# A gated mix of a state-space layer and a GELU layer: the opening's ScalarE table load and parameter rows are re-placed, and four loads are cut into pieces

## The chip, the cores and the metric

The kernel runs on one core of one Trainium2 chip. A core has five engines that run side by side and meet at semaphores: TensorE (PE in the profile; its weight loads are PEld), VectorE (DVE), ScalarE (ACT), GpSimd (POOL) and SyncE (SP). ScalarE and SyncE also issue DMA transfers, each into a queue of its own; "ACTq" and "SPq" are these issues in the profile. The metric is the device time in microseconds, the median of 9 runs of the kernel before: 217.02 us (216.68 to 217.1).

## The reference

Tokens `x` (2048 x 640, bfloat16) go through two branches, and a sigmoid gate per token mixes them. Branch A is a diagonal state-space layer: project the tokens to 640 complex states, scan over time, project back, add a skip. Branch B is a dense layer with tanh-GELU, 640 to 1728 to 640.

```python
x = A_x
g = _sigmoid((x * gate_w).sum(-1, keepdims=True))
# branch A
dt = jnp.exp(log_dt)
Lam_bar = jnp.exp(dt * Lam)
B_bar = ((Lam_bar - 1.0) / Lam)[:, None] * Bmat
Bu = jnp.einsum("bld,pd->blp", x + 0j, B_bar)
# for every t:  h = Lam_bar * h + Bu[:, t]
a = 2.0 * jnp.einsum("blp,dp->bld", hseq, Cmat).real + x * Dskip
# branch B
b = _gelu(x @ w1 + b1) @ w2 + b2
return g * a + (1 - g) * b
```

`log_dt`, `Lambda_re` and `Lambda_im` are the three parameter rows (640 values each) that the change is about.

## The kernel before, in words

The 2048 tokens are worked on in four chunks of 512, and a chunk in four strips of 128 tokens. All matmuls have 128 rows to contract, so the 640 features are five blocks (`KD`), the 640 states five (`KS`) and the 1728 hidden units thirteen full blocks and a rest of 64 (`KF` = 14).

**Main stages.** `ff1(c)` multiplies chunk c by `w1` (L251 through `ff1_mm`), and ScalarE takes the GELU (L256). `ssm(c)` multiplies it by B (L534); ScalarE copies the result out (L537) and VectorE does the rotation and the scan (L469, L488). `fin_b(c)` multiplies by `w2` (L592; the last 64 hidden units in L608, which read a transposed tile `gelL`), and `fin_a(c)` multiplies the scanned states by C (L651), after `seed` has put `x * Dskip` into the bank (L567). VectorE combines both into an output strip `ot` (L656), which SyncE stores (L665, the last one L663 on two queues). The list of calls at L670 to L694 sets the order of the chunks' stages. For TensorE, VectorE and ScalarE the order from line 168 on is the order in which the code is written (`manual_schedule`). What stands above line 168, and SyncE's queue throughout, is put in order by the framework, by priority and by a model of when things are ready: the load of token rows 2, written behind `fin_a(0)`, is issued in the trace behind the first of that stage's four stores.

**The opening.** Chunk 0 is not loaded transposed. Its four strips are loaded as they are (`load_xn(0, ...)`, L119, SyncE), TensorE turns each by a multiplication with the identity (`turn`, L216; five 128 x 128 blocks a strip), and VectorE (L223) and ScalarE (L225) copy the result into `xT[0]`. Of each strip VectorE copies blocks 0 to 2 and ScalarE blocks 3 and 4; these last two always go through the same PSUM bank, `pA`. So the next strip's blocks 3 and 4 can be written only when ScalarE has copied the strip before. Between the strips TensorE already multiplies what it has by the first columns of `w1` (`strip`, L251). `w1` comes as `w1a` (the first six blocks of hidden units; one tile for each of five feature blocks, of which ScalarE's queue loads feature blocks 0 and 2 and SyncE's the others) and `w1b` (the rest).

**Parameter rows.** Three small transfers of five rows of 128 values (`rows`, L125) put `log_dt`, `Lambda_im` and `Lambda_re` into the tile `prmA`, which VectorE has cleared. One matmul with the identity (L327, into `pA`, behind the twelfth `w1a` matmul of the opening's second round) turns them into columns, VectorE copies these into `colA` (L328), and from there a chain over ScalarE and VectorE makes the step dt, the angles and the sine and cosine tables (L329 to L422). The rows for b1 and the gate go into `prmB` by SyncE and are turned at L389.

**ScalarE's tables.** A function that is not in ScalarE's active table costs a table load. The kernel has three: for exp (asked for by a one-element activation on the tile `warm`, L210), for sine (L377) and for gelu (L256).

**Loads behind the opening.** SyncE issues, in this order, the `w1b` blocks (L143), B, chunk 1 and C as DMA transposes (L154 to L158), `w2` as one transfer of 2080 KB (L159), its last rows, the biases, chunks 2 and 3 as DMA transposes and the token rows of chunk 1 (L166, 640 KB). The token rows of chunks 2 and 3 are loaded later, by one transfer of 640 KB each, once the tile that they overwrite has been read.

Of the kernel before, what the change touches and what calls it, by code (L numbers as in the profile page):

```python
# [11 lines left out]
ACT = mybir.ActivationFunctionType  # L12
BF16 = mybir.dt.bfloat16
F32 = mybir.dt.float32
I32 = mybir.dt.int32

P = 128
# [6 lines left out]
KS = D // P  # L24
KF = (F + P - 1) // P
F_LAST = F - (KF - 1) * P
NT = T // P
TPC = CH // P
H = TPC // 2
# [12 lines left out]
def kernel(  # L42
# [19 lines left out]
    nc = tc.nc  # L62
# [4 lines left out]
    const = ctx.enter_context(tc.tile_pool(name="const", bufs=1))  # L67
# [7 lines left out]
    def bank(dtype=F32):  # L75
        return ps.tile([P, CH * 4 // (4 if dtype == F32 else 2)], dtype, name="bank")
# [7 lines left out]
    w2_sb = const.tile([P, KF - 1, D], BF16, name="w2_sb")  # L84
# [6 lines left out]
    prmA = const.tile([P, P], BF16, name="prmA")  # L91
# [23 lines left out]
    def load_xn(c, a0=0, a1=TPC, queue=None):  # L115
        if a0 == 0:
            xn[c] = xnp.tile([P, TPC, D], BF16, name="xn")
        r0 = c * CH + a0 * P
        (queue or nc.sync).dma_start(out=xn[c][:, a0:a1, :], in_=x2d[r0:r0 + (a1 - a0) * P, :].rearrange("(a p) d -> p a d", p=P))  # L119

    def load_w1a(queue, kd):
        queue.dma_start(out=w1a[kd][:], in_=B_w1[kd * P:(kd + 1) * P, 0:cut1])

    def rows(queue, dst, v):
        queue.dma_start(out=dst, in_=v.rearrange("(j p) -> j p", p=P))  # L125
# [2 lines left out]
    load_w1a(nc.scalar, 0)  # L128
    load_xn(0, 1, 2)
    load_w1a(nc.scalar, 2)  # L130
    load_xn(0, 2, 3)
    nc.vector.memset(prmA[:], 0.0)
    nc.vector.memset(prmB[:], 0.0)
    rows(nc.scalar, prmA[0:KS, :], A_log_dt)
    rows(nc.scalar, prmA[KS:2 * KS, :], A_Lambda_im)
    rows(nc.scalar, prmA[2 * KS:3 * KS, :], A_Lambda_re)
    load_xn(0, 3, 4)
    for kd in (1, 4, 3):
        load_w1a(nc.sync, kd)
    rows(nc.sync, prmB[KS:NB, :], B_b1[0:(KF - 1) * P])  # L140
# [15 lines left out]
    nc.sync.dma_start_transpose(out=xT[1][:], in_=x2d[CH:2 * CH, :])  # L156
    nc.sync.dma_start_transpose(out=CT_re[:], in_=A_C_re[:, :])
    nc.sync.dma_start_transpose(out=CT_im[:], in_=A_C_im[:, :])  # L158
    nc.sync.dma_start(out=w2_sb[:, 0:KF - 1, :], in_=B_w2[0:(KF - 1) * P, :].rearrange("(kf p) d -> p kf d", p=P))  # L159
    for h in range(2):  # L160
        nc.sync.dma_start(out=w2l[h * F_LAST:(h + 1) * F_LAST, :], in_=B_w2[(KF - 1) * P:F, :])
    nc.sync.dma_start(out=b2bc[:], in_=B_b2.rearrange("(o d) -> o d", o=1).to_broadcast([P, D]))
    nc.sync.dma_start(out=Dbc[:], in_=A_Dskip.rearrange("(o d) -> o d", o=1).to_broadcast([P, D]))
    nc.sync.dma_start_transpose(out=xT[2][:], in_=x2d[2 * CH:3 * CH, :])
    nc.sync.dma_start_transpose(out=xT[3][:], in_=x2d[3 * CH:4 * CH, :])
    load_xn(1)  # L166

    ctx.enter_context(tc.manual_schedule(engines={E.PE, E.DVE, E.Activation}))

# [36 lines left out]
    tf = const.tile([P, HC], F32, name="tf")  # L206
    nc.vector.tensor_copy(out=tf[:], in_=tfi[:])
    ones = lambda n: nc.const_aps.tensor(1.0, [P, n], BF16)
    warm = const.tile([P, 1], F32, name="warm")
    nc.scalar.activation(out=warm[:], in_=ones(1), func=ACT.Exp)  # L210
    pA = bank()
    for n in (512, 512, 512, 512, 512, 512, 128, 128):
        nc.tensor.matmul(pA[:, 0:n], lhsT=ones(P), rhs=ones(n), start=True, stop=True)
# [311 lines left out]
    def ssm(c, at={}):  # L525
        hs[c] = hsp.tile([P, 2 * KS, CH], BF16, name="hs")
        for ks in range(KS):
            if ks in at:
                at[ks]()
            bu = work.tile([P, 2, CH], BF16, name="bu", bufs=8)  # L530
            for ri, BT in enumerate((BT_re, BT_im)):
                p = bank()
                for kd in range(KD):
                    nc.tensor.matmul(p[:], lhsT=BT[ks >= KSA][:, kd, (ks % KSA if ks < KSA else ks - KSA) * P:][:, 0:P], rhs=xT[c][:, kd, :],  # L534
                                     start=(kd == 0), stop=(kd == KD - 1))
                    pe(CH)
                nc.scalar.activation(out=bu[:, ri, :], in_=p[:], func=ACT.Identity)  # L537
                act(0.6)
            scan_ops(c, ks, bu, ck.act)
            if c == 0 and ks == 0:  # L540
                later(0, 1.6, factors)
            let_out(ck.pe)
# [42 lines left out]
    def first_banks(c):  # L585
        biased(c, "wide", 0)
        biased(c, "wide", 1)
# [49 lines left out]
    def fin_a(c, at={}):  # L637
        let_out(0, c)
        for a in range(TPC):
            ti = c * TPC + a  # L640
            lo = a * P
            ot = fwork.tile([P, D], BF16, name="ot", bufs=2)
            if a < TPC - 2:
                seed(ti + 2)
            if a in at:
                at[a]()
            for i, (d0, d1) in enumerate(cuts(ti)):
                p = seeded[ti][i]
                for j in range(2 * KS):
                    CT = CT_re if j < KS else CT_im  # L650
                    nc.tensor.matmul(p[:, 0:d1 - d0], lhsT=hs[c][:, j, lo:lo + P], rhs=CT[:, j % KS, d0:d1],  # L651
                                     start=False, stop=(j == 2 * KS - 1), skip_group_check=True)
                    pe(d1 - d0)

                def f():
                    nc.vector.scalar_tensor_tensor(out=ot[:, d0:d1], in0=p[:, 0:d1 - d0], scalar=gcol[:, 0, ti:ti + 1],  # L656
                                                   in1=gbs[ti][:, d0:d1], op0=ALU.mult, op1=ALU.add)

                dve_now(ck.pe + 0.2, 0.45, f)
                if ti == NT - 1 and i > 0:  # L660
                    s0 = 0 if i == 1 else d0
                    q = nc.sync if i == 1 else nc.scalar
                    q.dma_start(out=out2d[ti * P:(ti + 1) * P, s0:d1], in_=ot[:, s0:d1])  # L663
            if ti < NT - 1:
                nc.sync.dma_start(out=out2d[ti * P:(ti + 1) * P, :], in_=ot[:])  # L665
# [12 lines left out]
    ff1(2, 0, {1: lambda: fold(3), 4: lambda: fold(4), 9: lambda: seed(0), 11: lambda: seed(1)})  # L678
    gates(2)
    fin_a(0)  # L680
    load_xn(2)
    ssm(2, {KS - 1: lambda: first_banks(1)})
    fin_b(1, seeds(1))
    fin_a(1)
    load_xn(3)
    ssm(3)
    gel_tile(3)
    ff1(3, 0, {KF - 3: lambda: first_banks(2)})
# [36 lines left out]
```

## Time and profile before

| what | value |
|---|---|
| median of 9 runs | 217.02 us |
| the profiled execution, device time | 216.84 us |
| its span, first to last instruction | 215.1 us |
| granted TensorE clock | 1.000 |
| TensorE: first matmul, first matmul on data (L216), last matmul's end | 0.77, 3.54, 211.7 us |
| DMA, mean over the span | 74 GB/s |
| DMA, 2.4 to 4.8 us | 332 to 380 GB/s |

From issue to landing, by tile: a strip of 160 KB took 3.3 to 3.6 us, a `w1a` block of 192 KB 2.7 to 3.6, a `w1b` block of 240 KB 3.4 to 5.9, `w2` 10.0, token rows of 640 KB 4.7 in the median.

How to read it: a busy share is an average over the span. What an edit is worth is read from the place that it touches, and there from the wait that ends last. "Idle before" in square brackets is the engine's idle time ahead of that instruction, with the work that ended it.

### The profile page before, as it was taken

How to read it: one execution, taken by the hardware profiler on the slowest of the kernel's cores; microseconds unless marked ns; L12 is line 12 of the kernel's file. 1: busy time of each engine (PE TensorE's matmuls, PEld its weight loads, DVE VectorE, ACT ScalarE, POOL GpSimd, SP SyncE). 2: the span in 40 equal slices, each digit the busy share in tenths (PEclk: the TensorE clock that was granted, in tenths of full speed). 3: DMA queues.
4: the chain of work that ended last, by engine and by line, in shares of the span. 5: the costliest groups of instructions: out<-in, count | busy, mean ns of one | idle time of the engine just before them, and what ended most of it. 6: DMA issues, size and time to landing. Idle time of an engine off the chain costs nothing.

```text
span 215.1 us, 3548 instructions
## 1 busy us (share of the span) xinstructions
PE 210.2 (98%) x1385; PEld 116.6 (54%) x1385; DVE 190.1 (88%) x396; ACT 101.1 (47%) x183; POOL 1.1 (0%) x12
## 2 busy tenths in 40 slices
PE   7999999999999999999999999999999999999993
PEld 4745444454454644775445677444445477654773
DVE  2799999999999999898999999999999999983252
ACT  2599556675876696203563210456682423204200
POOL 1000000000000000000000000000000000000000
PEclk9999999999999999999999999999999999999999
DMA  6899999990000000061000005100000000110011
GB/s 206 271 199 223 231 232 359 195 229 12 3 0 0 3 2 0 12 186 61 0 0 3 0 8 191 48 2 0 0 5 12 0 3 30 61 34 0 0 64 63
DMA packets 30323, 15.84 MB, mean 74 GB/s; under 512 B 22882, under 2 KB 30306, under 8 KB 30306
## 3 DMA queue, kind: packets, MB, share of 16 engines
q1 hardware_dynamic: 29844, 15.18, 28.3%
q10 hardware_dynamic: 462, 0.43, 0.6%
q8 instruction: 11, 0.18, 0.3%
q14 instruction: 6, 0.05, 0.1%
HBM read 7.48 MB, written 2.62 MB: 47 GB/s over the span
## 4 chain that ended last, share of the span: by engine, by line
PE 96%; DMA 1%; ACT 1%; DVE 0%; ACTq 0%; issue 0%
PE bank L592 26%; PE bank L251 26%; PE bank L651 20%; PE bank L534 20%; DMA xn<-in_A_x_dram 1%; PE bank L608 1%; PE bank L277 1%; ACT L210 1%; PE bank L216 0%; DVE ot L656 0%; ACT xT L225 0%; ACTq L125 0%; ACT warm L210 0%; PE bank L267 0%; PE bank L389 0%
## 5 line engine op out<-in xcount | busy, mean ns | idle before, releaser
L592 PE MATMUL bank<-w_sb,gel 128*128 128x512 bf16 (+1 forms) x416 | 57.9, 299 | 0.0
L592 PEld LDWEIGHTS <-gel 128*128 128x128 bf16 x416 | 32.2, 98 | 25.5
L537 ACT ACTIVATE bu<-bank 128x512 bf16<-128x512 f32 x40 | 23.9, 597 | 38.9 <-PE bank L534 38.8
L256 ACT ACTIVATE gel<-bank,colB 128x512 bf16<-128x512 f32 x52 | 34.0, 695 | 11.8 <-PE bank L251 11.1
L651 PEld LDWEIGHTS <-hs 128*128 128x128 bf16 x330 | 31.6, 98 | 11.5
L488 DVE TENSOR_TENSOR_SCAN g<-r_c,carry,v 128x512 bf16<-128x512 f32 x30 | 37.4, 1271 | 0.0
L600 ACT ACTIVATE gb<-bank,gcol 128x512 f32<-128x512 f32 (+1 forms) x32 | 15.1, 527 | 34.3 <-PE bank L608 18.1
L251 PE MATMUL bank<-xT,w1b 128*128 128x512 bf16 x140 | 31.0, 379 | 0.0
L251 PE MATMUL bank<-xT,w1a 128*128 128x512 bf16 (+1 forms) x156 | 27.4, 330 | 0.0
L651 PE MATMUL bank<-CT_re,hs 128*128 128x320 bf16 (+2 forms) x165 | 27.1, 295 | 0.0
L651 PE MATMUL bank<-CT_im,hs 128*128 128x320 bf16 (+2 forms) x165 | 27.1, 295 | 0.0
L656 DVE SCALAR_TENSOR_TENSOR ot<-bank,gcol,gb 128x320 bf16<-128x320 f32 (+2 forms) x33 | 17.5, 533 | 9.9 <-PE bank L651 8.7
L534 PE MATMUL bank<-xT,BT_im 128*128 128x512 bf16 x100 | 24.8, 379 | 0.0
L534 PE MATMUL bank<-xT,BT_re 128*128 128x512 bf16 x100 | 24.8, 379 | 0.0
L251 PEld LDWEIGHTS <-w1b 128*128 128x128 bf16 x140 | 13.7, 98 | 16.4
L251 PEld LDWEIGHTS <-w1a 128*128 128x128 bf16 x156 | 13.4, 98 | 12.5
L567 DVE TENSOR_TENSOR bank<-xn,Dbc 128x320 f32<-128x320 bf16 (+2 forms) x33 | 14.5, 480 | 2.8 <-ACT gb L600 2.7
L534 PEld LDWEIGHTS <-BT_im 128*128 128x128 bf16 x100 | 9.8, 98 | 11.8
L469 DVE TENSOR_TENSOR v<-wa,wb 128x512 bf16<-128x512 bf16 x40 | 15.2, 420 | 0.6
L534 PEld LDWEIGHTS <-BT_re 128*128 128x128 bf16 x100 | 9.7, 98 | 11.0
L581 ACT ACTIVATE bank<-b2bc 128x512 f32<-128x512 bf16 (+1 forms) x24 | 11.7, 529 | 7.0 <-DVE ot L656 7.0
L469 DVE TENSOR_TENSOR wa<-TCOS,g 128x1024 bf16<-128x1024 bf16 x20 | 13.7, 685 | 0.1
(100 smaller groups left out, 151.0 us busy)
## 6 DMA issues: line engine op xcount, KB each, us to landing
out_dram<-ot SPq DMA_DIRECT2D x15, 160.0 KB, 1.8
w_sb<-in_B_w_dram SPq DMA_DIRECT2D x1, 2080.0 KB, 10.0
xn<-in_A_x_dram SPq DMA_DIRECT2D x3, 640.0 KB, 4.7
w1b<-in_B_w_dram SPq DMA_DIRECT2D x5, 240.0 KB, 4.5
xn<-in_A_x_dram SPq DMA_DIRECT2D x4, 160.0 KB, 3.5
w1a<-in_B_w_dram SPq DMA_DIRECT2D x3, 192.0 KB, 2.9
w1a<-in_B_w_dram ACTq DMA_DIRECT2D x2, 192.0 KB, 3.3
w2l<-in_B_w_dram SPq DMA_DIRECT2D x2, 80.0 KB
```

Of the source, the lines that this page charges most:

```text
L251: nc.tensor.matmul(p[:, t0:t1], lhsT=w, rhs=xT[c][:, kd, t0:t1], start=(kd == 0) if first is None else first, stop=(kd == last), skip_grou ...
L256: nc.scalar.activation(out=gel[c][:, kf, :], in_=p[:, :], func=ACT.Gelu_apprx_tanh, bias=b1_c[:, kf:kf + 1])
L469: nc.vector.tensor_tensor(out=o, in0=a, in1=b, op=op)
L488: nc.vector.tensor_tensor_scan(s["g"][:, ri, :], r_c[:, ks:ks + 1].to_broadcast([P, CH]), s["v"][:, ri, :], init, ALU.mult, ALU.add)
L534: nc.tensor.matmul(p[:], lhsT=BT[ks >= KSA][:, kd, (ks % KSA if ks < KSA else ks - KSA) * P:][:, 0:P], rhs=xT[c][:, kd, :], start=(kd == 0 ...
L537: nc.scalar.activation(out=bu[:, ri, :], in_=p[:], func=ACT.Identity)
L567: dve_now(ck.pe, 0.45, lambda: nc.vector.tensor_tensor(out=p[:, 0:d1 - d0], in0=xn[c][:, a, d0:d1], in1=Dbc[:, d0:d1], op=ALU.mult))
L581: nc.scalar.activation(out=v, in_=src, func=ACT.Identity)
L592: nc.tensor.matmul(p[:, col:col + d1 - d0], lhsT=gel[c][:, kf, a * P:(a + 1) * P], rhs=w2_sb[:, kf, d0:d1], start=False, stop=False, skip_ ...
L600: nc.scalar.activation(out=gbs[ti][:, d0:d1], in_=p[:, col:col + d1 - d0], func=ACT.Identity, scale=gcol[:, 1, ti:ti + 1])
L651: nc.tensor.matmul(p[:, 0:d1 - d0], lhsT=hs[c][:, j, lo:lo + P], rhs=CT[:, j % KS, d0:d1], start=False, stop=(j == 2 * KS - 1), skip_group ...
L656: nc.vector.scalar_tensor_tensor(out=ot[:, d0:d1], in0=p[:, 0:d1 - d0], scalar=gcol[:, 0, ti:ti + 1], in1=gbs[ti][:, d0:d1], op0=ALU.mult, ...
```

## The change

Three things are changed.

- The one-element exp activation that calls up ScalarE's first table stands behind ScalarE's two `w1a` loads; it stood at line 210, behind the three parameter rows.
- The three parameter rows are issued by SyncE, behind the fourth strip and ahead of its `w1a` blocks; they were issued by ScalarE.
- `w2` comes in four transfers (blocks 0 to 2, 3 to 5, 6 to 8 and 9 to 12), and the token rows of chunks 1, 2 and 3 in two halves each. Six transfers are added in all, each of them on SyncE's queue; the bytes are the same.

```diff
     load_w1a(nc.scalar, 0)
     load_xn(0, 1, 2)
     load_w1a(nc.scalar, 2)
+    warm = const.tile([P, 1], F32, name="warm")
+    nc.scalar.activation(out=warm[:], in_=nc.const_aps.tensor(1.0, [P, 1], BF16), func=ACT.Exp)
     load_xn(0, 2, 3)
     nc.vector.memset(prmA[:], 0.0)
     nc.vector.memset(prmB[:], 0.0)
-    rows(nc.scalar, prmA[0:KS, :], A_log_dt)
-    rows(nc.scalar, prmA[KS:2 * KS, :], A_Lambda_im)
-    rows(nc.scalar, prmA[2 * KS:3 * KS, :], A_Lambda_re)
     load_xn(0, 3, 4)
+    rows(nc.sync, prmA[0:KS, :], A_log_dt)
+    rows(nc.sync, prmA[KS:2 * KS, :], A_Lambda_im)
+    rows(nc.sync, prmA[2 * KS:3 * KS, :], A_Lambda_re)
     for kd in (1, 4, 3):
         load_w1a(nc.sync, kd)
...
-    nc.sync.dma_start(out=w2_sb[:, 0:KF - 1, :], in_=B_w2[0:(KF - 1) * P, :].rearrange("(kf p) d -> p kf d", p=P))
+    for k0, k1 in ((0, 3), (3, 6), (6, 9), (9, KF - 1)):
+        nc.sync.dma_start(out=w2_sb[:, k0:k1, :], in_=B_w2[k0 * P:k1 * P, :].rearrange("(kf p) d -> p kf d", p=P))
...
-    load_xn(1)
+    for a in (0, H):
+        load_xn(1, a, a + H)
...
-    warm = const.tile([P, 1], F32, name="warm")
-    nc.scalar.activation(out=warm[:], in_=ones(1), func=ACT.Exp)
...
     fin_a(0)
-    load_xn(2)
+    load_xn(2, 0, H)
+    load_xn(2, H, TPC)
...
     fin_a(1)
-    load_xn(3)
+    load_xn(3, 0, H)
+    load_xn(3, H, TPC)
```

## The prediction

> **What bounds the kernel now.** I read the page first, for the shares of the engines and the chain that ended last:
>
> ```profile
> PE 210.2 (98%) x1385; PEld 116.6 (54%) x1385; DVE 190.1 (88%) x396; ACT 101.1 (47%) x183; POOL 1.1 (0%) x12
> ...
> PE 96%; DMA 1%; ACT 1%; DVE 0%; ACTq 0%; issue 0%
> ```
>
> TensorE (PE) is busy for 210.2 of the 215.1 us. The stretches of the span show the rest: 0.77 us before its first matmul, 3.4 us after its last (211.7 to 215.1), which leaves about 0.73 us idle in between. Whatever does not move TensorE's work cannot move the end. Next, the chain of waits in order of time, to find those 0.73 us:
>
> ```profile
> 3.52 0.26 ACTq L125
> 3.78 0.03 issue
> 3.81 1.28 ACT L210
> 5.09 0.01 issue
> 5.11 0.20 ACT warm L210
> 5.31 0.28 ACT xT L225
> 5.59 0.04 issue
> 5.63 0.27 PE bank L216 x2
> ```
>
> Before these lines the chain holds the first token strip's transfer (0.72 to 3.49). From there to 5.63 it runs over ScalarE: the issue of the third parameter row (L125), which waited for that strip; behind it the table load (1.28 us), the warm-up and the copy of the first strip's transposes (L225). The timelines of ScalarE, then of TensorE, show what stands in line there and who waits for it:
>
> ```profile
> 1.66 0.57 ACTq L125 DMA_DIRECT2D prmA<-in_A_log_dt_dram  x1
> 2.26 0.27 ACTq L125 DMA_DIRECT2D prmA<-in_A_Lambda_im_dram  x1
> 3.52 0.26 ACTq L125 DMA_DIRECT2D prmA<-in_A_Lambda_re_dram  x1
> 3.81 1.28 ACT L210 ACT_TABLE_LOAD   x1 [3.81 <-DMA xn<-in_A_x_dram]
> 5.11 0.20 ACT L210 ACTIVATE warm<-const-bfloat16-1.0 128x1 f32<-128x1 bf16 x1
> 5.21 0.36 ACT L225 ACTIVATE xT<-bank 128x256 bf16<-128x256 f32 x1
> ```
>
> ```profile
> 4.57 0.34 PE L216 MATMUL bank<-ident,xn 128*128 128x128 bf16 x3
> 5.63 0.27 PE L216 MATMUL bank<-ident,xn 128*128 128x128 bf16 x2 [0.72 <-ACT xT L225]
> 5.74 0.83 PE L251 MATMUL bank<-xT,w1a 128*128 128x128 bf16 x12
> 6.41 0.17 PE L327 MATMUL bank<-ident,prmA 128*128 128x15 bf16 x1
> ```
>
> The reader is to see one stall of 0.72 us: TensorE, ready at 4.91, may not write the second strip's transposes into `pA` before ScalarE has copied the first strip's out of it. That is practically all of TensorE's idle time. The last line matters as much: L327 turns the three parameter rows into columns, and TensorE stands there in order until all three rows have landed.
>
> **The table load moves.** ScalarE's two `w1a` issues end at 1.62 (0.72 plus 0.90). Table load at 1.65 to 2.93, warm-up 2.95 to 3.15: over before the first strip's transposes finish at 4.23 (3.54 plus 0.69), so nothing waits for it; the cover is the wait for the first strip. The copy L225 then runs at 4.27 to 4.63 and is done before TensorE wants `pA`: three transposes of the second strip start at 4.57, one each 0.063 us, so the next two start at 4.76 and end 0.27 later, at 5.03. ScalarE copies them at 5.07 to 5.45. Without anything else L327 could come when 12 matmuls are issued; the last six of them need the first of VectorE's two copies (L223, two from 4.95 in 0.62, so about 5.25 to 5.3) and take half of the 0.67 us that lies between 5.74 and 6.41. That gives 5.63 instead of 6.41: 0.78 us earlier.
>
> On a table load row and rule differ. In this trace the load takes 1.28 us and the warm-up follows 0.02 us behind. The Trainium skill ("ScalarE: Activation LUTs", section "What ACT_TABLE_LOAD costs") counts a drain of about 1.38 us on top, 2.66 in all. By that figure ScalarE would be free at about 4.5, the first copy would end at about 4.9, and L327 would be possible some 0.15 later: still not what decides, by the next part.
>
> **The three rows move to SyncE.** ScalarE loses three issues (0.57, 0.27, 0.26 us), all hidden or gone with the stall. SyncE issues its four strips from 0.72 to 2.54 and stood idle until 3.69, as its timeline shows:
>
> ```profile
> 0.72 1.82 SPq L119 DMA_DIRECT2D xn<-in_A_x_dram  x4
> 3.69 1.65 SPq L122 DMA_DIRECT2D w1a<-in_B_w_dram  x3
> ```
>
> Rows one and two fit in that hole: 2.58 to 3.15 and 3.2 to 3.47. The third cannot be issued at once. The semaphore numbers in the DMA records cycle over eight, and an issue waits for the transfer that had its number eight issues before: that is why the third row waited for strip one, and why SyncE's first `w1a` issue waited 1.1 us for the `w1a` block that ScalarE had asked for (landed 3.68 by its completion events). With six issues on SyncE ahead of them the third row takes that place: I expect it at 3.69 to 3.95. Behind it in SyncE's queue the first `w1a` block slips 0.3 us (to 3.99); the next ones do not, since the second waited for strip two anyway (landed 4.52, issued 4.54). The slipped block lands at 6.4 to 6.8 and is first read after 9 us. Everything SyncE issues later, the b1 and gate rows, `w1b` and the transposes, keeps its time.
>
> Landing of the third row: before, issued at 3.52, its completion events end at 5.67, so 2.15 us. Issued at 3.69 it lands at 5.85. Bounds: its packets now stand behind strip four on the same queue, whose completions come at 5.17 to 5.70; on ScalarE's queue the rows landed one after another at 4.92, 5.30 and 5.67, about 0.37 apart. If a further such step comes on top, 6.2; if the path is a little quicker, 5.6. From landing to matmul it was 0.04 and 0.05 us for strip one, so L327 at 5.95, with 5.65 to 6.32 as ends. I take 5.95, nearest to the like row. So TensorE gives back about 0.3 of the 0.78 us as a new wait at L327.
>
> **Sum.** 6.41 minus 5.95 is 0.46 us. From L327 on the work is linked: VectorE's `colA` copy, the next write to `pA`, dt, the table chain (8.64, 10.0, the sine table load, 12.4), then the gelu table load and the first gelu, all follow it. Strips three and four (landed 5.32 and 5.70) are wanted at 6.1 and 7.3. So I shift all by 0.46. What does not shift are transfers. The nearest is the fifth `w1b` block: issue at 8.0, longest landing 5.9, so 13.9, and its weights were loaded at 14.54; after the shift 14.08. Covered by 0.17; if that cover is gone, at most 0.3 us come back. Next come the first matmuls of `ssm(0)` at 21.5 whose four B transposes land at 15.1 to 21.1 by their completion events, each 4 us and more ahead of its use.
>
> **More pieces.** `w2` in four issues instead of one: three more of 0.59 us on SyncE at 29 to 31. The whole block landed 10.0 us after 29.00 and is first read at 57.5. Behind it on SyncE stand `w2l`, the bias, Dskip, two transposes, token rows 1 and the first gelu transpose; they slip 2 us and a few more where an issue now waits for a `w2` piece. The earliest user is L608 at 64.75, with its transpose issued at 44.4. So nothing: it would take a slip of 10 us and more before a us of it is seen. Token rows of chunks 2 and 3 in halves: one more issue of 0.39 us each at 92.4 and 128.9, and an output store that may slip by as much. VectorE already waits for such a store (0.63 us at 97.29); TensorE does not wait for VectorE there, and no matmul there starts closer than 0.8 us behind the work it needs. If that cover were gone, 0.4 us each. I take nothing. The skill speaks against pieces ("DMA: Bandwidth & Descriptors", "Rules for kernel authors": at least 1 MiB per transfer for bandwidth). In this trace 160 and 192 KB transfers moved 332 to 380 GB/s between 2.4 and 4.8 us; and even at half the rate of before (an estimate) `w2` would land by 49 to 50, ahead of 57.5: nothing by either.
>
> The profiled execution took 216.84 us (span 215.1, 1.7 around it): 216.84 minus 0.46 is 216.38. It lies 0.18 under the median of 217.02, so the median becomes **216.56 us**.
>
> **Rivals.**
> *The rows are in time.* L327 at 5.63 to 5.7, gain 0.72 to 0.78, 216.24 to 216.3. For it: two rows are out by 3.5. Against it: the third needs another 2.15 us from 3.69.
> *The wait moves to the rows or to `w1b`.* The rows land a step late each, or `w1b` eats the rest: gain 0 to 0.1 or a loss of 0.2; 216.9 to 217.2. For it: the 0.37 steps above, and strip four ahead in the queue. Against it: those rows were shared with a queue full of strips, and theirs is nearly empty after 5.
> *Slower: the table load gets ahead of ScalarE's issues.* The schedule is pinned only from line 168 on. If load and warm-up stand before the first `w1a` issue, that block lands up to 1.5 us later, at 5.2; the third row, which waits for it, lands 2.15 later, 7.35; L327 at 7.45, 1.05 later than now: 218.1. Between the two issues it costs about 0.5. It decides as soon as the first issue starts after about 2. For it: SyncE's order is not the code's (token rows 2 stand after four stores in the code and are issued behind the first). Against it: ScalarE's five issues stand in code order in the trace.
> *It does not do what it says* is the second rival with the stall at 4.91 unchanged: only if the load stayed behind a wait for a strip.
>
> **Chances.** Forecast 0.60 (own range 216.2 to 216.95), rows in time 0.14, moved wait 0.12, slower 0.14. About 0.2%, 0.43 us, can be told from no change: faster means under 216.59. The forecast lies just below that line, so 0.33 of its 0.60, plus 0.14: 0.47. Same: 0.27 plus 0.12. Slower 0.14. The range goes from 216.15, full gain and a little, to 217.2, the end of the moved wait; the slower rival stays out.
>
> **What would show it.** Table load at about 1.65; no ScalarE wait at L216; a new TensorE wait of about 0.3 us ahead of L327 put down to a row's transfer; L327 near 5.95; the second gelu stage shifted alike, and TensorE's last matmul near 211.2. It is wrong if L327 comes after 6.3, if a wait appears at `w1b` near 14, or if any matmul after 27 us waits for a transfer or VectorE.

## The result, and the profile after

The changed kernel takes **216.23 us** (median of 10 runs, 215.81 to 216.77), against 216.97 us for the kernel before (median of 30). The ratio is 0.9969, with a 95% interval of 0.9961 to 0.9977: faster by 0.31%. The forecast was 216.56, with a range of 216.15 to 217.2 that holds the time. Its profiled execution took 216.08 us, span 214.3 (before 216.84 and 215.1), so 0.76 us are to be found.

The chain that ended last, by engine, and ScalarE's and SyncE's timelines of the changed kernel (start, duration, engine, line; in brackets the idle time ahead and what ended it; from here on lines are those of the kernel shown: L218 was L216, L253 was L251, L329 was L327):

```profile
PE 98%; DVE 0%; issue 0%
```

```profile
1.66 1.28 ACT L132 ACT_TABLE_LOAD   x1 [1.66 <-PEq L713]
2.95 0.20 ACT L132 ACTIVATE warm<-const-bfloat16-1.0 128x1 f32<-128x1 bf16 x1
4.33 0.38 ACT L227 ACTIVATE xT<-bank 128x256 bf16<-128x256 f32 x1 [1.17 <-PE bank L218]
```

```profile
2.60 0.37 SPq L125 DMA_DIRECT2D prmA<-in_A_log_dt_dram  x1
3.01 0.26 SPq L125 DMA_DIRECT2D prmA<-in_A_Lambda_im_dram  x1
3.73 0.26 SPq L125 DMA_DIRECT2D prmA<-in_A_Lambda_re_dram  x1
4.03 1.79 SPq L122 DMA_DIRECT2D w1a<-in_B_w_dram  x3
```

ScalarE's part of the chain is gone. Load, warm-up and the first and third row issue stand within 0.04 us of where the prediction put them; the second row went out 0.19 us earlier than predicted (3.01 for 3.2), since the first issue took 0.37 us and not 0.57. TensorE's timeline in the opening, with one line of before ahead of it:

```profile
4.21 0.50 PE L251 MATMUL bank<-xT,w1a 128*128 128x128 bf16 x6
```

```profile
3.58 0.71 PE L218 MATMUL bank<-ident,xn 128*128 128x128 bf16 x5
4.24 0.80 PE L253 MATMUL bank<-xT,w1a 128*128 128x128 bf16 x6
5.02 0.71 PE L218 MATMUL bank<-ident,xn 128*128 128x128 bf16 x5
5.53 0.93 PE L253 MATMUL bank<-xT,w1a 128*128 128x128 bf16 x12
6.29 0.17 PE L329 MATMUL bank<-ident,prmA 128*128 128x15 bf16 x1
```

No wait of 0.72 us stands at L218 any more, and yet L329 starts at 6.29, only 0.12 ahead of before (6.41). The durations say why: the first six w1a matmuls took 0.50 us before (L251) and 0.80 now (L253).

The chains in order of time agree that 0.12 is all that reaches VectorE's last combine. Their last lines, of before, then of after:

```profile
200.78 10.91 PE bank L651 x90
211.68 0.03 issue
211.71 0.35 DVE ot L656
```

```profile
200.66 10.90 PE bank L653 x90
211.56 0.03 issue
211.59 0.35 DVE ot L658
```

The other 0.64 us lie behind it, where the prediction never looked. Behind the last stores SyncE runs five closing waits, each for two semaphores, and then a drain; the other engines' last closing records come behind that drain. A transfer counts up a semaphore as it lands, and eight semaphores are used in turn. These are its last records in the trace, before and after (place in SyncE's stream counted from one, start in us, time since the record before ended, the semaphores waited for; the two last stores carry 100 and 103 before, 109 and 110 after):

```
before                                         after
77 211.971 0.045 wait 105, 104                 86 211.853 0.046 wait 105, 104
78 212.041 0.042 wait 106, 103                 87 211.923 0.042 wait 106, 103
   103 full at 213.60                          88 211.989 0.038 wait 108, 100
79 213.661 0.043 wait 107, 100                 89 213.195 1.178 wait 109, 102
80 214.158 0.469 wait 108, 102                    110 full at 213.47
81 214.237 0.051 wait 109, 110                 90 213.483 0.260 wait 110, 107
82 214.307       drain                         91 213.548       drain
```

The reader is to see two things. Before, the last landing released the second wait of five; three more followed, and a pause of 0.47 us ahead of the 80th record: 0.71 us from landing to drain. After, it released the last wait: 0.08 us. Six more transfers have moved the last stores on by six in the cycle of eight semaphores, so to the end of SyncE's list, and the 80th record lies at 204.79, among earlier stores, where SyncE has time.

So the profiled gain is 0.12 in the opening and 0.64 at the end, 0.76 in all. The experiments test that split.

### The profile page after: what moved, and what is told of

It is laid out like the page before. It is cut to its first block, busy times and chain, and to the rows that moved or that the text cites. A ratio compares the mean times of both kernels' runs of the same rounds, so it can differ in the third digit from the quotient of the medians.

```text
span 214.3 us, 3555 instructions
## 1 busy us (share of the span) xinstructions
PE 210.8 (98%) x1385; PEld 117.1 (55%) x1385; DVE 190.2 (89%) x396; ACT 101.2 (47%) x183; POOL 1.1 (0%) x12
## 3 DMA queue, kind: packets, MB, share of 16 engines
HBM read 7.48 MB, written 2.62 MB: 47 GB/s over the span
## 4 chain that ended last, share of the span: by engine, by line
PE 98%; DVE 0%; issue 0%
PE bank L253 27%; PE bank L594 27%; PE bank L653 20%; PE bank L536 20%; PE bank L215 1%; PE bank L610 1%; PE bank L279 1%; PE bank L218 1%; DVE ot L658 0%; PE bank L269 0%; PE bank L391 0%; PE bank L329 0%
## 5 line engine op out<-in xcount | busy, mean ns | idle before, releaser
L253 PE MATMUL bank<-xT,w1b 128*128 128x512 bf16 x140 | 31.0, 379 | 0.0
L253 PE MATMUL bank<-xT,w1a 128*128 128x512 bf16 (+1 forms) x156 | 27.8, 334 | 0.0
L253 PEld LDWEIGHTS <-w1b 128*128 128x128 bf16 x140 | 13.7, 98 | 16.5
L253 PEld LDWEIGHTS <-w1a 128*128 128x128 bf16 x156 | 13.7, 100 | 12.5
```

Source lines behind the costliest of these rows:

```text
L253: nc.tensor.matmul(p[:, t0:t1], lhsT=w, rhs=xT[c][:, kd, t0:t1], start=(kd == 0) if first is None else first, stop=(kd == last), skip_grou ...
```

## The experiments

Each profiled execution is split in three: the start of L327 (L329), from there to the end of VectorE's last combine, and from there to SyncE's drain. About 0.75 us of the span come behind (0.87 in "minus two"). A number given for L327 is that of L329 or L328 where the kernel's lines have moved. "Transpose" is the start of the first strip's first transpose. "Clock" is the start of the long full-rate stretch in the trace's clock records. Behind the first two rows come three groups of four kernels, each run on one chip together with the kernel before, which had medians of 217.10, 217.09 and 217.11 us there.

| kernel | clock | transpose | L327 | L327 to last combine | to drain | median | ratio to before, 95% |
|---|---|---|---|---|---|---|---|
| before | 4.08 | 3.54 | 6.41 | 205.65 | 2.25 | 216.97 | |
| changed | 5.71 | 3.58 | 6.29 | 205.65 | 1.61 | 216.23 | 0.9969, 0.9961 to 0.9977 |
| opening alone | 5.79 | 3.52 | 6.22 | 205.65 | 2.46 | 217.16 | 1.0000, 0.9986 to 1.0015 |
| pieces alone | 4.85 | 3.55 | 6.42 | 205.65 | 1.61 | 216.23 | 0.9960, 0.9946 to 0.9974 |
| plus two | 4.97 | 3.50 | 6.37 | 205.65 | 2.33 | 217.16 | 1.0009, 0.9992 to 1.0026 |
| rows early | 5.00 | 3.49 | 5.94 | 206.39 | 1.59 | 216.29 | 0.9954, 0.9938 to 0.9970 |
| changed, again | 5.47 | 3.67 | 6.17 | 205.65 | 1.59 | 216.03 | 0.9954, 0.9936 to 0.9971 |
| pieces alone, again | 4.79 | 3.62 | 6.49 | 205.77 | 1.62 | 216.58 | 0.9990, 0.9973 to 1.0007 |
| rows early, again | 4.93 | 3.58 | 5.93 | 206.65 | 1.58 | 216.26 | 0.9959, 0.9946 to 0.9972 |
| plus eight | 6.40 | 3.74 | 6.86 | 205.65 | 1.80 | 216.71 | 0.9983, 0.9969 to 0.9998 |
| minus two | 4.29 | 3.55 | 6.41 | 206.00 | 2.03 | 216.90 | 0.9981, 0.9961 to 1.0001 |
| no warming | 8.59 | 3.52 | 6.60 | 206.24 | 1.59 | 216.92 | 0.9984, 0.9963 to 1.0005 |
| old place of warm | 4.77 | 3.51 | 6.02 | 205.66 | 1.58 | 216.01 | 0.9938, 0.9916 to 0.9960 |
| pieces alone, third | 3.39 | 3.81 | 6.67 | 205.65 | 1.61 | 216.45 | 0.9962, 0.9942 to 0.9981 |

("Old place of warm" has no clock record; there its value is the first pair of matmuls of 128 columns at the full rate.)

### The change in two halves

The opening alone leaves out these edits, and the pieces alone are these edits in the kernel before (the token rows of chunks 1 and 3 are halved in the same way):

```diff
-    nc.sync.dma_start(out=w2_sb[:, 0:KF - 1, :], in_=B_w2[0:(KF - 1) * P, :].rearrange("(kf p) d -> p kf d", p=P))
+    for k0, k1 in ((0, 3), (3, 6), (6, 9), (9, KF - 1)):
+        nc.sync.dma_start(out=w2_sb[:, k0:k1, :], in_=B_w2[k0 * P:k1 * P, :].rearrange("(kf p) d -> p kf d", p=P))
...
-    load_xn(2)
+    load_xn(2, 0, H)
+    load_xn(2, H, TPC)
```

> The change without its pieces: warm-up activation behind ScalarE's two w1a issues, rows on SyncE, w2 and token rows as before. Theory END (most of the gain comes at the end of the program: the last two stores' semaphores stand in the last two of SyncE's five closing waits in the changed kernel, and in the second and third before): without the six transfers the last stores have their old semaphores, so from the last store's landing to SyncE's drain about 0.7 us as before, not 0.08; the gain is that of the opening alone, 0.1 to 0.5 us, 216.5 to 216.9. Theory OPENING (the prediction's: all of the gain lies in the opening): 0.46 to 0.75 us, 216.2 to 216.5, with the end as in the changed kernel.

> The kernel before with the six added transfers alone. END: the last stores take the last two semaphores, landing to drain 0.1 us instead of 0.7, so 0.6 us faster, 216.3 to 216.45; the stall of 0.72 us ahead of L216 is still there. OPENING: no change, 216.9 to 217.0.

The pieces alone take 216.23 us, a gain of 0.87, and the opening alone 217.16, none, where 216.5 to 216.9 was expected. TensorE's timeline with the pieces alone still has the stall of before:

```profile
4.81 0.36 PE L218 MATMUL bank<-ident,xn 128*128 128x128 bf16 x3
5.64 0.27 PE L218 MATMUL bank<-ident,xn 128*128 128x128 bf16 x2 [0.47 <-ACT xT L227]
5.75 0.83 PE L253 MATMUL bank<-xT,w1a 128*128 128x128 bf16 x12
6.42 0.17 PE L329 MATMUL bank<-ident,prmA 128*128 128x15 bf16 x1
```

So the step of the prediction that priced the pieces at nothing is refuted. The opening alone did bring 0.19 us (6.22), and its end grew by 0.21. With the rows' three issues SyncE's stream is three records longer than before, so its 80th record falls ahead of the first closing wait, at 212.21. An instruction transfer is the third line among the DMA queues from 211 to 216 us (packets, MB, share of 16 engines; the changed kernel has none there, and that of the kernel before starts at 214.78, behind the last landing):

```profile
q1 hardware_dynamic: 144, 0.13, 7.9%
q10 hardware_dynamic: 144, 0.03, 3.0%
q14 instruction: 1, 0.01, 0.6%
```

It runs from 212.83 to 213.33. Of ScalarE's last store (q10) nine packets start only at 213.33, where the others have started by 213.03, and its sixteenth completion event comes at 214.07, the other fifteen by 213.48. I read this as a part of the store held up by the transfer of instructions; only the times speak for it, and it was seen in this one profile.

### Rank and pause at the end

Plus two (w2 in three transfers, the last stores in the first closing wait), plus eight (w2 in nine; the same semaphores as before) and minus two (no loads of b2 and Dskip):

```diff
+    for k0, k1 in ((0, 5), (5, 9), (9, KF - 1)):
```

```diff
+    for k0, k1 in ((0, 2), (2, 4), (4, 6), (6, 8), (8, 9), (9, 10), (10, 11), (11, 12), (12, KF - 1)):
```

```diff
-    nc.sync.dma_start(out=b2bc[:], in_=B_b2.rearrange("(o d) -> o d", o=1).to_broadcast([P, D]))
-    nc.sync.dma_start(out=Dbc[:], in_=A_Dskip.rearrange("(o d) -> o d", o=1).to_broadcast([P, D]))
+    nc.gpsimd.memset(b2bc[:], 0.0)
+    nc.gpsimd.memset(Dbc[:], 0.0)
```

> The kernel before with w2 in three transfers, two more in all: the last two stores' semaphores move into the first of the five closing waits. END: four waits and the drain stand behind the last landing instead of three; landing to drain 0.7 to 0.8 us, so 0 to 0.1 us slower than before, 216.9 to 217.1. Rival within END (the 0.47 us gap between the third and fourth closing wait belongs to a place in SyncE's program and not to the waits): the gap may lie under the long wait now, 0.3 to 0.4 us faster. OPENING: no change.

> The kernel before with w2 in nine transfers, eight more in all and the same number modulo eight, so the last stores stay on the semaphores of the kernel before, the second and third of SyncE's five closing waits; the fixed pause of 0.47 us in SyncE's stream moves eight places towards the front, among the waits for earlier stores. Theory (two parts: the rank of the semaphores, and the pause): last landing to drain about 0.24 us, a gain of 0.45, 216.5 to 216.65. Rival (the rank alone is what counts): 0.7 us from landing to drain and the time of before, 217.0. Rival (finer pieces as such): as fast as the six extra transfers, 216.2.

> The kernel before with two transfers less: the bias row b2 and the skip row are zero-filled by GpSimd in place of being loaded, so both terms are left out of the output. Two less is the same modulo eight as six more, so the last stores stand on the last two of SyncE's closing waits as in the changed kernel; but SyncE's stream has two places less ahead of the end, and the fixed pause (0.47 us ahead of the 80th record) falls between the last wait and the drain. Theory (rank and pause are two things): last landing to drain 0.5 to 0.6 us, 0.1 to 0.2 less than before, 216.9. Rival (the rank alone): 0.08 us, and 0.6 less than before, 216.45. The stall at the second strip stays, L327 at 6.4.

From the last landing to the drain: plus two 0.79 us, plus eight 0.25, minus two 0.50. SyncE's last records in the two that tell rank and pause apart:

```
plus eight                                     minus two
86 212.496 0.041 wait 106, 103                 77 212.486 0.042 wait 107, 100
   103 full at 214.06                          78 213.661 1.147 wait 108, 102
87 214.117 0.039 wait 107, 100                    109 full at 213.94
88 214.181 0.036 wait 108, 102                 79 213.958 0.269 wait 109, 110
89 214.243 0.034 wait 109, 110                 80 214.441 0.455 drain
90 214.308       drain
```

Both parts are shown: the rank (which of the five waits the last landing releases) costs 0.17 us (0.25 less 0.08), the pause 0.47, together the 0.64 that the changed kernel saves. Finer pieces as such show no worth: plus two gains nothing, and plus eight, with the finest pieces, gains 0.38, less than six do and 0.07 less than expected. Its profiled execution took 216.85 us: there the opening was 0.45 us later than before, under a clock that opened at 6.40, and used up what the end had gained. Minus two came out at 216.90 as expected, though its interval touches 1; it also lost 0.35 us between L327 and the end, 0.2 of it in a wait for `w1b`.

### What limits the opening now

The first kernel here leaves out the eight warming matmuls ahead of the first strip.

> The changed kernel without the eight warming matmuls at the start, whose result nothing reads. Theory (TensorE runs at half rate until its clock opens, and that limits the opening once ScalarE's stall is gone): from the first transpose to L329 everything at 0.107 us a matmul of 128 columns, L329 between 6.3 and 6.5, the half rate goes on to somewhere between 7 and 10.5, and the end comes 0.6 to 2.3 later than in the changed kernel: 216.8 to 218.4. Rival (the late second strip and the rows set L329): L329 at 6.1 to 6.3 as in the changed kernel, 216.0 to 216.3.

```diff
-    for n in (512, 512, 512, 512, 512, 512, 128, 128):
-        nc.tensor.matmul(pA[:, 0:n], lhsT=ones(P), rhs=ones(n), start=True, stop=True)
```

> The changed kernel without one of its edits: the warming activation stays at its old place in the code. With the rows gone from ScalarE's queue nothing stands ahead of the table load there but the two w1a issues. Theory: table load at 1.66 all the same, no stall at the second strip, L329 between 5.95 and 6.4, the same time as the changed kernel. Rival (the edit in the code is needed): table load at 3.8, stall of 0.5 to 0.7 at the second strip.

This second kernel, "old place of warm", is the row part of the change and the six pieces, without the moved lines of `warm`.

Without the warming the kernel takes 216.92 us, 0.91 more than the kernel beside it with the same opening. TensorE's timeline there:

```profile
4.19 0.80 PE L251 MATMUL bank<-xT,w1a 128*128 128x128 bf16 x6
4.79 0.74 PE L216 MATMUL bank<-ident,xn 128*128 128x128 bf16 x5
5.32 1.48 PE L251 MATMUL bank<-xT,w1a 128*128 128x128 bf16 x12
6.60 0.22 PE L327 MATMUL bank<-ident,prmA 128*128 128x15 bf16 x1
```

Its matmuls of 128 columns start 0.107 us apart up to 8.55, and 0.055 apart from 8.63 on; L327 at 6.60 is a little behind the 6.3 to 6.5 expected. In the changed kernel the same step lies at 5.7, in the repeat at 5.5, in "old place of warm" at 4.8, in the kernel before between 3.94 and 4.21. It moves from run to run with nothing in the kernel to move it, and it is the half rate that shows as 0.80 for six matmuls. In the kernel before the full rate had come before those six. With the old opening a later clock cost nothing up to 4.97, since TensorE stood waiting for ScalarE until 5.59 or later: L327 comes 2.87 us behind the first transpose in all six profiles whose clock opened between 3.39 and 4.97.

"Old place of warm" has, on every engine, the same working instructions in the same order as the changed kernel: with nothing but two issues ahead of it on ScalarE the load comes at 1.65 either way, and that edit is empty. Its time, 216.01, agrees with the repeat of the changed kernel, 216.03. Its clock opened early, and here the third row does what the prediction said. TensorE's timeline, then what its weight loads waited for from 3 to 7 us (total, times, longest):

```profile
5.05 0.93 PE L253 MATMUL bank<-xT,w1a 128*128 128x128 bf16 x12
6.02 0.18 PE L329 MATMUL bank<-ident,prmA 128*128 128x15 bf16 x1
```

```profile
PEld L329 <- DMA prmA<-in_A_Lambda_re_dram: 0.2, 1, 0.2
```

The row landed at 5.97, and L329 followed 0.05 later, 0.39 earlier than before.

### The opening's worth, with the good end on both sides

> The changed kernel once more, for a second profile and a time next to the kernels of this call. Theory (the gain lies at the end, where the last stores now stand on the last semaphores that SyncE waits for; the opening gives 0.1 to 0.2): 216.2 to 216.4, the last store's landing to the end of SyncE's drain about 0.08 us as in the first profile, and L329 between 5.95 and 6.4, by when the clock opens. Rival (the first profile's short end was chance): an end of 0.3 us or more after the last landing.

> The six extra transfers alone once more, beside the whole change. Theory: the same end (0.08 us behind the last landing), the stall at the second strip's transposes still there (0.5 to 0.7), L329 at 6.4; slower than the whole change by what the opening gives, 0 to 0.2 us. Rival (the opening's part is worth the 0.46 us that I had forecast and the first pair of times hid it): slower than the whole change by 0.4 or more.

> The six extra transfers alone, a third time, beside a kernel with the new opening and the same end (the one without the edit to the warming activation). Theory: L329 at 6.4 to 6.5 against 6.0 to 6.4, so 0.1 to 0.4 us slower than that kernel, the end behind the last landing 0.08 us in both. Rival: no difference between the two, or 0.5 us and more as in the second pair of times.

The changed kernel is faster than the pieces alone by 0.55 us in one pair (216.03 against 216.58) and by 0.44 in the other ("old place of warm" at 216.01 against 216.45). The profiles of the two pairs show 0.32 and 0.66 us at L329, of which 0.30 in the second is a first strip that landed later. Measured from the first transpose, L329 comes 2.87 us later with the old opening (six profiles, clock from 3.39 to 4.97), 2.70 and 2.72 with the new one where the clock opens at 5.7 or later, and 2.50 and 2.51 where it opens sooner. With the clock at 6.40 (plus eight) the old opening takes 3.12. So the opening brings 0.15 to 0.17 or 0.36 to 0.37 us by the profiles. The medians are too coarse to say more: against the kernel before as measured beside them, the pieces alone gained 0.87, 0.51 and 0.66 us in three measurements, and the changed kernel 0.74 and 1.06. In the first of each the pieces alone gained more than the whole change, so that the opening is worth half a us is not shown.

### Rows earlier still

```diff
     load_xn(0, 1, 2)
...
+    rows(nc.sync, prmA[0:KS, :], A_log_dt)
+    rows(nc.sync, prmA[KS:2 * KS, :], A_Lambda_im)
+    rows(nc.sync, prmA[2 * KS:3 * KS, :], A_Lambda_re)
     load_xn(0, 2, 3)
...
     load_xn(0, 3, 4)
-    rows(nc.sync, prmA[0:KS, :], A_log_dt)
-    rows(nc.sync, prmA[KS:2 * KS, :], A_Lambda_im)
-    rows(nc.sync, prmA[2 * KS:3 * KS, :], A_Lambda_re)
```

> The changed kernel with the three rows issued between strips 2 and 3 instead of behind strip 4. If the rows' landing limits L329 in the opening: rows land near 5 us, L329 at 5.6 to 5.8, 0.3 to 0.5 us faster than the changed kernel, 215.7 to 215.95. If strip 2 or the second w1a block lands late there (4.97 and 5.17 in the profile of the changed kernel, 4.52 and 4.71 before) and that limits: 0 to 0.15 us faster, 216.1 to 216.25. If strip 4, issued behind the first w1a block's landing, comes late: L218 waits for it near 7, and some of it is lost again.

> The whole change with the parameter rows between the second and the third strip, once more. Theory: L329 about 5.9 to 6.0, so 0.2 to 0.4 us less than the whole change unless the clock opens late; the 0.5 us that TensorE waited at L653 in the first profile came from one late landing and does not come again: 215.9 to 216.1. Rival (the opening's time is lost again further on, at a place that does not move): the same as the whole change, with the 0.5 us at L653 or another wait of that size.

L329 came at 5.94 and 5.93, 0.23 to 0.36 earlier than in the two profiles of the changed kernel, and the time is not better: 216.26 beside 216.03. The gain was lost twice, at two places. In the first profile VectorE waited 1.8 us for an output store at some 97 us, and TensorE 0.50 us for VectorE at 177.85. In the second TensorE waited for a `w1b` block. VectorE's wait from 95 to 101 us and TensorE's timeline in the first, then TensorE's timeline in the second:

```profile
DVE ot L658 <- DMA out_dram<-ot: 1.8, 1, 1.8
```

```profile
177.85 0.84 PE L653 MATMUL bank<-CT_re,hs 128*128 128x320 bf16 x5 [0.50 <-DVE bank L569]
```

```profile
15.27 1.04 PE L253 MATMUL bank<-xT,w1b 128*128 128x512 bf16 x4 [0.83 <-DMA w1b<-in_B_w_dram]
```

That block landed at 15.22; in the changed kernel all five were there by 13.62 in one profile and by 14.24 in the other. That the wait at 177.85 comes from the one at 97 is argued, not shown: VectorE is busy nearly all the time between. I had expected that such a wait doesn't come again. It did, elsewhere, so no version here beats the changed kernel.

## Why the prediction was right, and where not

**Right: faster, and inside the range.** That is in good part luck. Of the 0.74 us of the medians the prediction had 0.46 by name, and in the profile of the result its mechanism brought 0.12; the other 0.64 came from a term that it took as nothing. Of its signs, the table load at 1.65 or 1.66 and the vanished stall came in every profile of the new opening. A wait for a row came in one, of 0.2 us, and TensorE's last matmul ended at 211.56, not near 211.2.

**"More pieces ... I take nothing": failed.** All that was said of `w2` and the token rows holds: TensorE waits for no transfer after 27 us, and the cost is hidden. What was left out is that a transfer is also a place in the cycle of semaphores and in SyncE's stream. I used that cycle to date the third row at the start of the program and didn't follow it to the last store. The first view of the prediction had the room for it: 3.4 us between the last matmul and the end of the span, taken as fixed ("Whatever does not move TensorE's work cannot move the end"). That sentence is wrong by 0.64 us.

**"6.41 minus 5.95 is 0.46 us": the right mechanism, too large.** L329 came at 6.29, 6.17 and 6.02, all inside the bounds 5.65 to 6.32, for a gain of 0.12 to 0.39. The third row landed at 6.08, 5.97 and 5.97 in these three (5.85 forecast), and in the last it was the wait. In the others it was TensorE at half rate: the prediction counted its matmuls with the durations of before, where the full rate had come by 4.21. In the first profile the second strip was late as well: its last completion event came at 4.97, fifteen of sixteen by 4.29.

The Trainium skill ("TensorE: Matmul & The Clock Gate", Part 1, on the HAM clock gate) says that the array runs at half clock until a free-running window of some 3.4 us has been busy, so that the number of slow matmuls varies from run to run of one kernel. The traces agree on the two rates, 0.107 and 0.055 us from start to start, and on the spread, with an opening between 3.39 and 6.40 us in the thirteen profiles with the warming matmuls. They don't bear out the length of the window: the earliest opening lies 2.62 us behind the first warming matmul (0.77).

**"I shift all by 0.46": the rigid shift is shown.** From L327 to the last combine nine of the profiles have 205.65 to 205.66 us, whatever the opening did. No wait at `w1b` appeared near 14 in the changed kernel. But the 0.17 of cover rested on a longest landing of 5.9 us, and that was too short: the fifth block took 5.16 and 6.18 us from issue in the two profiles of the changed kernel and 6.96 in "rows early, again", where TensorE waited 0.83. The forecast's "at most 0.3 us" for a lost cover was too little. Nor does it take a shift: in "minus two", with the old opening, the block took 6.99 us and TensorE waited 0.2.

**The table load.** 1.66 for 1.28 us, warm-up 0.01 behind, nothing waits for it: as worked out. That the warm-up had to be moved for it was not so.

**The rivals.** "The rows are in time" came nearest in time (216.24 to 216.3) for a reason that isn't its own: no profile of the changed kernel's order of issues had the rows in time for 5.7 (third row at 5.83 to 6.08 in five). The table load didn't get ahead of ScalarE's issues, so the slower rival fell. "The wait moves" happened in part, to TensorE's own rate and not to the rows.

## What to carry to other kernels

Look at what stands behind the last store: which of the closing waits its semaphore is, and what of the queue's own stream falls between the landing and the drain; one transfer more or less, far ahead of the end, moves both. Test an edit with several parts in parts, and compare each from the same landmarks (here L327, last combine, drain), because an end can hide what an opening gains, as the 0.21 us at the end of the opening alone hid its 0.19. And where a stall goes, ask what ran slowly under its cover: here a TensorE at half rate that cost nothing with the old opening.

## What the runs showed of the hardware that I had not expected

- SyncE pauses for 0.46 to 0.47 us ahead of the 80th record of its stream, whatever that is: a wait in the kernel before and with the opening alone, the drain with minus two. Where the record itself waits longer for something else, as the store's issue with the pieces alone does (2.32 us), the pause doesn't show by itself. An instruction transfer of 8 KB follows 0.62 to 0.64 us after that record's start in most of the profiles that show the pause (before 214.16 and 214.78; changed 204.79 and 205.43; minus two 214.44 and 215.07), and 0.91 us after it in "rows early, again". That SyncE fetches its next block of instructions there is my reading; nothing here shows the cause.
- Each further closing wait takes 0.06 to 0.08 us although its semaphores have long been full.
- The table of busy time by stretch gives a granted TensorE clock of 1.00 from 3.4 to 6.5 us without the warming matmuls, where every matmul ran at half rate. The spacing of equal matmuls tells the rate; that column doesn't.
- The same load, the fifth `w1b` block, took 5.16 us from issue to its last completion event in one profile (8.46 to 13.62) and 6.96 in another (8.26 to 15.22), with the DMA transposes of B behind it on the same queue.
